# A fused block-causal attention and gated FFN kernel: the float32 first piece goes from 192 to 384 tokens, with q and k bounds on ScalarE and another DMA model in the planner

## The chip, the cores and the metric

The kernel runs on one core of a Trainium2 chip. TensorE (PE) does matrix products into PSUM, VectorE (DVE) and ScalarE (ACT) element-wise work and reductions, GpSimd (POOL) small element-wise work, and SyncE (SP) issues all DMAs. The metric is the device time of one execution in microseconds, lower is better. PEld in a profile is the loading of weights into TensorE, which runs beside its matmuls.

## What is computed

Eight sequences of 576 tokens go through attention with 8 heads of 64, masked by blocks of 64 tokens (a block of queries sees its own and all earlier blocks of keys). The heads are put side by side to 4608 x 512, and a feed-forward layer of width 2048 with the gate h * clip(h + 3, 0, 6) / 6 follows.

```python
scores = scale * np.matmul(q, k.transpose(0, 1, 3, 2))
mask = block_i >= block_j
scores = np.where(mask, scores, -1000000000.0)
scores = scores - np.max(scores, axis=-1, keepdims=True)
attn = np.exp(scores)
attn = attn / (np.sum(attn, axis=-1, keepdims=True) + 1e-09)
x = np.matmul(attn, v) ...
h = x @ w_in
g = h * np.clip(h + 3.0, 0.0, 6.0) / 6.0
return g @ w_out
```

q, k and v are float32. The two weights come as 64-bit numbers, which the kernel takes as pairs of 32-bit words.

## The kernel before

**Precision.** Most products are made from float16 pairs: an operand is scaled by a power of two and split into a high and a low float16 part, and three of the four partial products are summed (hi x hi, hi x lo, lo x hi). An f16 matmul covers half the output rows (64) and is issued in pairs for the two halves. The power of two comes from a bound on the operand's magnitude, made by `pow2_scale` (line 518) out of per-partition values in `mx`, which a matmul with ones sums over the partitions.

**The weights.** Each of the 8 chunks (`NCH`) of the two weight matrices is loaded in four quarters by `w_load` (594). Each quarter lies in one of three raw buffers and is turned to float32 in place by four operations: a sign (`sg`, line 622, VectorE or POOL), an exponent (`ex`, 623) and two bit operations on VectorE. `WX` (line 23) says up to which quarter the third raw buffer lies in x buffer 1, behind which it is `pT01`. The float32 form of chunk c lies where the f16 form of chunk c+1 will be, the last one in x buffers 2 and 3. `w_max` (637) finds the magnitudes and `w_split` (650) makes the f16 parts. A split of chunk c overwrites float32 weights of chunk c-1, so it comes behind the float32 FFN steps up to 2c (`splits`, line 1330).

**Batch 0 is computed in float32.** For each of its four pairs of heads, `qk_load32` and `qk_prep32` bring and transpose q and k, `s_block32` makes the scores of one block of 64 queries for both heads (matmul, maximum on VectorE, exponential on ScalarE), `t_block32` transposes the probabilities on TensorE and copies them out of PSUM, and `pv_group32` (940) does three blocks together: reciprocal sums, `rd` (36 multiplies of 64 columns in all, on POOL, line 948), a matmul `pr` that spreads them over partitions, a copy `rb`, the product with v and the scaling. The first group of three blocks (tokens 0 to 191, T0) of all four pairs goes to `x32`, float32; the other two groups (tokens 192 to 575) are split to f16 into x buffer 1.

**Batches 1 to 7** take f16 pairs: 28 slots, one for each batch and pair of heads (n = 4 to 31). `qk_prep` (758) finds the bounds of q and k with one maximum reduction (`absmax`, line 762) on VectorE, scales, splits and transposes by DMA. `s_group` (988) makes scores, maxima `st`, multiplies them with the scale (line 1033, VectorE), takes exponentials on ScalarE, splits the probabilities to `phl`, and a transposing DMA (`t_dma`) brings them to `pT`. `pv_group` (1102) multiplies with v and splits into x buffers.

**The FFN runs over pieces of tokens** (`pieces`, line 1088): piece 0 is (batch 0, tokens 0 to 191) in float32, piece 1 (0, 192 to 575), piece 2 (1, 0 to 383), piece 3 (1, 384 to 575), and then nine pieces of 384 tokens for six batches. A piece has 16 steps f of 128 hidden columns. `ffn1` makes `h` and the gate `g`, and `ffn2` adds to the accumulators `o0` to `o2` (one bank of PSUM for each 128 tokens), `LAG` (3) steps behind. In float32 a step is 4 products h over the piece's tokens, and one product of 512 columns for each 128 tokens, or two half-height ones of 256 columns for the last 64.

**What sets the order.** Nothing is emitted as it is called. A `Recorder` (line 84) notes every operation with its tiles and a due time `key`, and `schedule` (260) simulates the five engines with a cost formula (`cost`, 205), choosing at each engine's free moment the ready operation with the earliest due time; the resulting order is then fixed for each engine. A few operations may go to several engines ("AV" is ScalarE or VectorE, "VPA" any of three), and the planner chooses. Due times come from the constants at the top: `AS` and `U` for the first blocks of batch 0 and `TA`, `PV0` behind them, `RT`, `RS`, `TR` for the others, `W0 + i * WD` for the weight quarters, `S0`, `SD` for the splits, `AT` for the f16 slots and `FT` for the FFN pieces, with `PVA` and `PVB` placing the two value products of a slot. A DMA's landing is modelled in lines 423 to 426, where plain DMAs share one queue and transposes do not enter it.

PSUM has eight banks: three `s` (scores, value products, small matmuls), two `h`, and `o0` to `o2`, which the float32 attention also uses for transposes until the FFN needs them (`EVP`, `PRO`).

Of the kernel before, what the change touches and what calls it, by code (L numbers as in the profile page):

```python
# [17 lines left out]
P = 128  # L18
# [3 lines left out]
LAG = 3  # L22
WX = 10
WY = 27

U = 2.788
AS = (7.494, 11.408, 15.3, 22.633)
AL = 14.807
PV0 = 2.519
TA, TR, PR = 2.197, 5.661, 0.677  # L30
QR = 3.417
PVA, PVB = 0.93, 1.25
PHS = 18
# [4 lines left out]
EVR = 3  # L38
EVP = 2
PRO = True  # L40
MEM = 0

NMIN = 64
QL = 0.849
VL = 0.2
W0, WD = 4.938, 2.891
S0, SD = 57.576, 4.59
M0, MD = 34.073, 5
RT = (25.619, 42.369, 59.881, 71.242)
RS, RL, VL1 = 2.796, 15.216, 24.0  # L50
VM0, VMX = 10.452, 0.3
AT = ((4, 86.25), (6, 128.63), (8, 159.32), (10, 199.92), (12, 240.31), (14, 287.79), (16, 335.13), (24, 565.96), (32, 826.62))
FT = ((0, 28), (1, 100), (2, 168.81), (3, 239.13), (4, 279.57), (5, 356.87), (7, 505.16), (10, 740.96), (13, 988.23))
QP = 0.55
# [23 lines left out]

ADV = {("tensor", "a"): 60.0}


class Recorder:
# [4 lines left out]
    NAMES = ("tensor", "vector", "scalar", "gpsimd", "sync")  # L89
    LAT = {"tensor": 55, "vector": 37, "scalar": 39, "gpsimd": 65, "sync": 65}  # L90
    TURN = 95
    BIAS = {"vector": 250.0, "gpsimd": 500.0}
# [67 lines left out]
    def add(self, ways):  # L160
        eng, method, args, kw = ways[0]
        outs, ins = self.operands(args, kw)
        last = self.ops[-1] if self.ops else None
        if eng == "tensor" and self.joint is not None and last and last.joint == self.joint:
            op = last
            calls, occ, _, _ = op.ways[eng]
            more, took, _ = self.cost(eng, method, args, kw, outs, ins)
            op.ways[eng] = (calls + [(method, args, kw)], occ + more, occ + took, False)
        else:
            op = Op()  # L170
            op.joint, op.n, op.ways = None, len(self.ops), {}
# [12 lines left out]
    def touch(self, op, a, w):
# [18 lines left out]
        self.hist[t.name] = keep  # L203

    def cost(self, eng, method, args, kw, outs, ins):


        n = self.count(outs[0])
        if method == "dma_start":
            nb = mybir.dt.size(outs[0].dtype)  # L210
            for _, c in list(outs[0].ap):
                nb *= c
            if kw.get("transpose"):
                occ = max(1290, 172 * nb / 32768 - 150)
                return occ, occ + (1100 if nb <= 4 * 32768 else 2100), False
            if eng == "gpsimd":
                return 1300, 2900 + nb / 170, False
            return 600, 2000 + nb / 170, False
# [17 lines left out]
        if eng == "scalar":  # L236
            occ = 94 + 0.8335 * n
            if isinstance(kw.get("scale"), bass.AP):
                occ += 95
            if isinstance(kw.get("bias"), bass.AP):  # L240
                occ += 58
            if "accum_out" in kw:
                occ += 93
            return occ, occ + 105, False
        if eng == "gpsimd":
# [14 lines left out]
    def schedule(self):  # L260
# [63 lines left out]
        while done < N:  # L324
# [96 lines left out]
            while head < N and ops[head].start is not None:  # L421
                head += 1
            if calls[0][0] == "dma_start" and not calls[0][2].get("transpose"):
                nb = (took - (2900.0 if e == "gpsimd" else 2000.0)) * 0.8
                dma = max(dma, o.end - nb - 400.0) + nb
                o.end = max(o.end, dma + 400.0)
            now[e] = t + occ
# [7 lines left out]
            for s, flow in succ[pick]:  # L435
                rs = ready[s]
                for q in rs:
                    r = t if q == e and (e == "tensor" or not flow) else o.end + self.LAT[q]
                    rs[q] = max(rs[q], r)
                ndep[s] -= 1  # L440
                if not ndep[s]:
                    for q in rs:
                        heapq.heappush(pend[q], (rs[q], s))
# [12 lines left out]
def kernel(  # L456
# [31 lines left out]
    NGB, NPB, NST_B = ((4, 5, 4), (3, 6, 3), (3, 5, 5))[MEM]  # L488
    T0 = GT
    NTA, NTR = 2, 3  # L490

# [266 lines left out]
    def qk_prep(n):  # L758
        t = qn.pop(n)
        mx = sm.tile([P, 2], F32, tag="qkmx", name=f"qkmx{n}")  # L760
        sp = attp.tile([P, 3, NST, 2, D], F16, tag="qks", name=f"qks{n}", bufs=1)
        absmax(mx, t)
        pw, rs = pow2_scale(mx, 2, f"q{n}")
# [28 lines left out]
    def qk_load32(n):  # L792
        t = attp.tile([P, 2, NTA, 2, D], F32, tag="vhl", bufs=2, name=f"qf{n}")
        qn[n] = t
        for s, src in enumerate((q, k)):
            nc.sync.dma_start(t[:, s, 0], src[0, 2 * n:2 * n + 2, :P].rearrange("h p d -> p h d"))
            nc.sync.dma_start(
                t[:BLK, s, 1], src[0, 2 * n:2 * n + 2, P:T0].rearrange("h p d -> p h d")
            )

    def qk_load32_rest(n):
        t = natp.tile([P, 2, NTR, 2, D], F32, tag="qk", bufs=2, name=f"qr{n}")
        for s, src in enumerate((q, k)):
            for h in range(2):
                nc.sync.dma_start(
                    t[:, s, :, h], src[0, 2 * n + h, T0:].rearrange("(t p) d -> p t d", p=P)
                )
        qn[n] = t

    def qk_prep32(n, rest):  # L810
# [29 lines left out]
        for s in (1, 0):  # L840
            if rest and not QTH:
                ps = ps_s.tile([P, 512], F32, tag="s", name=f"qt{n}_{s}r")
            else:
                ps = ps_h.tile([P, S - T0], F32, tag="h", name=f"qt{n}_{s}")
            for u in range(NTR if rest else NTA):
# [62 lines left out]
    def t_block32(n, i):  # L908
# [7 lines left out]
        if ii == 0:  # L916
            tag = "pT2" if g or n in (1, 2) else "pT01"
            pT[n, g] = attp.tile(
                [P, PT_U[g], P], F32, tag=tag, bufs=2 if tag == "pT2" else 1, name=f"pT{n}_{g}"
            )  # L920
        t = pT[n, g]
        for u0 in range(0, nu, 4):
            u1 = min(u0 + 4, nu)
            full = u1 - 1 if half and u1 == nu else u1
            if g == 0 or EVP >> len(n_ev) % 3 & 1:
                o = 2 if g else len(n_ev) % 3
                pp = ps_o.tile([P, 4, P], F32, tag=f"o{o}", name=f"pt{n}_{i}_{u0}")
# [12 lines left out]
    def pv_group32(n, g):  # L940
# [6 lines left out]
        for i in range(GB):  # L947
            nc.gpsimd.tensor_scalar(rd[:, i], ident2, r[:, i:i + 1], 1.0, op0=ALU.mult, op1=ALU.mult)
        if g == 0 or PRO:
            o = 2 if g else len(n_ev) % 3  # L950
            pr = ps_o.tile([P, GT], F32, tag=f"o{o}", name=f"pr{n}_{g}")
# [5 lines left out]
        nc.scaled(rb, pr, 1.0, "AV")  # L957
        if g == 0:
            ps = ps_h.tile([P, GT], F32, tag="h", name=f"pf{n}_{g}")
        else:  # L960
            ps = ps_s.tile([P, GT], F32, tag="s", name=f"pf{n}_{g}")
        nj = (3 * g + 2) // 2 + 1
        for j in range(nj):
# [4 lines left out]
            for h in range(2):  # L968
# [6 lines left out]
                )  # L975
        if g == 0:
            nc.vector.tensor_mul(x32[:, n, :T0], ps, rb)
            return
        nc.vector.tensor_mul(rb, ps, rb)
        rs = vscale[0][1][:, 0:1]  # L980
        x = xb[1]
        xs = slice((g - 1) * GT, g * GT)
        nc.scaled(x[:, 0, n, xs], rb, rs, "AV")
# [4 lines left out]
    def s_group(n, g):  # L988
# [19 lines left out]
        for si, some in enumerate(banks):  # L1008
# [22 lines left out]
            if len(some) > 1:  # L1031
                nc.vector.tensor_tensor(st[:, 2:3], st[:, 2:3], st[:, 3:4], op=ALU.min)
            nc.vector.tensor_scalar_mul(st[:, 4 + i0:4 + i1], st[:, i0:i1], sc[:, 0:1])
            for ii, c0, c1, rg in regions:
# [52 lines left out]

    pieces = [[(b, *r)] for b in range(2) for r in ((0, (T0, TP)[b]), ((T0, TP)[b], S))]
    for b in range(2, B, 2):
        pieces += [[(b, 0, TP)], [(b, TP, S), (b + 1, 0, GT)], [(b + 1, GT, S)]]  # L1090
# [273 lines left out]
    for n in range(NPAIR):  # L1364
# [3 lines left out]
        at(t, qk_prep32, n, 0)  # L1368
        for i in range(GB):
            at(t + (1 + i) * U, s_block32, n, i)  # L1370
            at(t + (1 + i) * U + TA, t_block32, n, i)
        at(t + GB * U + TA + PV0, pv_group32, n, 0)

    for n in range(NPAIR):
# [3 lines left out]
        at(AS[3] + 0.1 + 0.1 * n, v_max, n)  # L1378
        for i in range(2 * GB):
            at(t + i * RS, s_block32, n, GB + i)  # L1380
            at(t + i * RS + TR, t_block32, n, GB + i)
        for g in (1, 2):
            at(t + (g * GB - 1) * RS + TR + PR, pv_group32, n, g)

# [88 lines left out]
```

## Time and profile before

| | |
|---|---|
| median of 3 runs | 1059.81 us (1059.1 to 1061.09) |
| span of the profiled execution | 1063.1 us |
| busy: PE | 995.4 us (94%), 11588 matmuls |
| busy: PEld | 726.0 us (68%) |
| busy: DVE | 833.9 us (78%) |
| busy: ACT | 635.8 us (60%) |
| busy: POOL | 75.9 us (7%) |
| mean granted TensorE clock | 0.980 |
| DMA share over the span | 61.4% of 16 engines, 127 MB |

In the profile, tiles are named as in the program with buffer numbers left out: `h`, `o`, `s`, `pv` are PSUM tiles of the matmuls; `sf`, `pt`, `pr`, `pf` those of the float32 attention; `pf` is also the name of its probabilities. All operations have the line of the recorder's caller (L452), so groups are told apart by tile and form. A form "128*64 128x384 f16" of a matmul is 128 rows by 64 columns of weights and 384 moving columns. A row of the list of waits reads: engine and tile that waited, what released it, us in total, times, longest. A row of a group reads: form and count, then busy us and mean ns of one, then idle time of the engine ahead of them and what ended most of it. A timeline row reads: start, length of the merged stretch, and in brackets idle time ahead and its releaser.

### The profile page before, as it was taken

The page shows a single profiled execution, that of the slowest core. Times are in us where ns is not written, and L with a number is a line of the kernel's source. Part 1 is how long each engine was busy: PE and PEld are TensorE (multiplying, and loading weights), DVE is VectorE, ACT ScalarE, POOL GpSimd, SP SyncE. Part 2 cuts the span into 40 slices and gives each one's busy share as a digit, 9 for nine tenths or more (in the row PEclk, how much of TensorE's full clock was granted, in tenths as well). Part 3 has the DMA queues.
Part 4 walks back from the last instruction along what each step waited for, and adds up shares of the span by engine and source line. Part 5 has one row for each costly group of instructions (what it writes and reads, how often), then busy time and mean ns, then how long its engine had stood idle before and what let it go on. Part 6 is the DMA issues. An engine that isn't in the chain of part 4 may idle for free. (4 is left out here: it accounts for less than half of the span.)

```text
span 1063.1 us, 28968 instructions
## 1 busy us (share of the span) xinstructions
PE 995.4 (94%) x11588; PEld 726.0 (68%) x11588; DVE 833.9 (78%) x2308; ACT 635.8 (60%) x1548; POOL 75.9 (7%) x259
## 2 busy tenths in 40 slices
PE   6978967999999999999999999999999999999998
PEld 4645646776777867667766666777767777777776
DVE  4888999999999999899899889787898875332322
ACT  4668757666657676666776565566556563343332
POOL 3132220000000000000000000000000000000000
PEclk8998988999999999999999999999999999999999
DMA  6756546898889887888888779647656533000000
GB/s 157 189 166 180 141 111 140 140 185 156 152 159 171 153 152 143 147 164 149 156 143 181 133 116 167 118 77 143 117 90 128 92 80 57 1 31 2 31 1 31
DMA packets 414199, 128.90 MB, mean 121 GB/s; under 512 B 403184, under 2 KB 403440, under 8 KB 414064
## 3 DMA queue, kind: packets, MB, share of 16 engines
q1 hardware_dynamic: 414064, 127.05, 61.4%
q8 instruction: 91, 1.49, 0.6%
q14 instruction: 44, 0.36, 0.1%
HBM read 45.09 MB, written 9.44 MB: 51 GB/s over the span
## 5 line engine op out<-in xcount | busy, mean ns | idle before, releaser
L452 PE MATMUL h<-x,win 128*64 128x384 f16 (+2 forms) x4720 | 437.0, 321 | 1.8 <-DVE win L452 1.6
L452 PE MATMUL o<-wout,g 128*64 128x512 f16 (+3 forms) x3444 | 430.9, 381 | 2.2 <-DVE g L452 2.2
L452 PEld LDWEIGHTS <-win 128*64 128x64 f16 x4608 | 296.8, 110 | 69.9 <-issue 2.2
L452 PEld LDWEIGHTS <-g 128*64 128x64 f16 x3360 | 221.6, 110 | 105.9 <-issue 2.0
L452 ACT ACTIVATE r<-h,eg,sh 128x384 f32<-128x384 f32 (+1 forms) x240 | 137.1, 593 | 131.5 <-PE h L452 130.8
L452 ACT ACTIVATE p<-s,st,esc 128x64 f32<-128x64 f32 (+1 forms) x280 | 163.1, 587 | 73.6 <-DVE st L452 53.6
L452 DVE SCALAR_TENSOR_TENSOR r<-r,eg,h 128x384 f32<-128x384 f32 (+1 forms) x192 | 113.4, 592 | 116.1 <-ACT r L452 116.0
L452 DVE SCALAR_TENSOR_TENSOR phl<-p,st,phl 128x128 f16<-128x128 f32 (+4 forms) x252 | 135.3, 582 | 0.7 <-ACT phl L452 0.6
L452 ACT ACTIVATE g<-r 128x384 f16<-128x384 f32 (+1 forms) x165 | 84.5, 513 | 85.8 <-DVE r L452 84.9
L452 DVE SCALAR_TENSOR_TENSOR g<-r,g 128x384 f16<-128x384 f32 (+1 forms) x192 | 102.7, 535 | 29.9 <-ACT g L452 29.4
L452 DVE TENSOR_REDUCE st<-s 128x1 f32<-128x64 f32 (+1 forms) x280 | 120.0, 447 | 4.1 <-PE s L452 3.8
L452 PE MATMUL s<-qkT 128*64 128x64 f16 (+7 forms) x1120 | 99.0, 289 | 10.0 <-ACT p L452 6.4
L452 PEld LDWEIGHTS <-vhl 128*64 128x64 f16 x1680 | 72.3, 111 | 41.2 <-issue 25.3
L452 PE MATMUL pv<-pT,vhl 128*64 128x192 f16 (+2 forms) x1680 | 75.1, 235 | 24.8 <-DMA pT<-phl 20.8
L452 ACT ACTIVATE phl<-p,st 128x256 f16<-128x256 f32 (+4 forms) x135 | 70.4, 556 | 34.4 <-DVE st L452 18.7
L452 PEld LDWEIGHTS <-qkT 128*64 128x64 f16 x1120 | 60.0, 111 | 35.4 <-issue 13.0
L452 POOL MEMSET p<- 128x64 f32 x140 | 21.4, 154 | 521.4 <-DVE phl L452 492.5
L452 ACT ACTIVATION_READ_ACCUMULATOR p<-s,st,esc 128x1 f32 x280 | 55.1, 197 | 0.0
L452 DVE TENSOR_SCALAR phl<-p,st 128x512 f16<-128x512 f32 (+4 forms) x117 | 46.0, 424 | 1.8
L452 DVE SCALAR_TENSOR_TENSOR qks<-qk,rs_q,qks 128x576 f16<-128x576 f32 x56 | 44.7, 817 | 0.0
L452 ACT ACTIVATE x<-pv 128x192 f16<-128x192 f32 (+1 forms) x61 | 22.0, 360 | 33.4 <-PE pv L452 30.7
L452 DVE TENSOR_REDUCE qkmx<-qk 128x2 f32<-128x1152 f32 x28 | 37.6, 1344 | 1.6 <-DMA qk<-in_k_dram 1.6
(154 smaller groups left out, 819.4 us busy)
## 6 DMA issues: line engine op xcount, KB each, us to landing
out_dram<-osb SPq DMA_DIRECT2D x35, 256.0 KB, 2.5
vnat<-in_v_dram SPq DMA_DIRECT2D x64, 128.0 KB, 2.9
qk<-in_q_dram SPq DMA_DIRECT2D x28, 288.0 KB, 3.6
qk<-in_k_dram SPq DMA_DIRECT2D x28, 288.0 KB, 4.4
rawo<-in_moe_w_out_dram SPq DMA_DIRECT2D x15, 512.0 KB, 4.6
rawi<-in_moe_w_in_dram SPq DMA_DIRECT2D x14, 512.0 KB, 4.0
pT<-phl SPq DMA_TRANSPOSE x140, 3.4
vnat<-in_v_dram SPq DMA_DIRECT2D x32, 32.0 KB, 2.7
```

The source lines that it names most:

```text
L452: getattr(eng, method)(*args, **kw)
```

## The change

The float32 piece takes two groups of three blocks of each pair instead of one: T0 is 384, and G32 = 2 counts those groups. Piece 0 is (0, 0 to 383), piece 1 the remaining 192 tokens of batch 0 in f16; the later pieces are the same. The first load of a pair brings three tiles of 128 tokens, the second 192 tokens, and the buffers of the two change places. The groups 0 and 1 of a pair share one `pT` tile; both use the `o` banks for transposes and `pr` and the `h` bank for the value product, the third group uses `s` banks alone. The x split remains for the third group. `rd` goes to ScalarE or VectorE. `qk_prep` takes the sum of magnitudes per partition, by two ScalarE passes with an accumulator, in place of one maximum on VectorE. The product of `st` and the scale may go to ScalarE or VectorE. The planner gets one queue for all DMAs, with lead, tail and rate for loads, stores and transposes; a matmul that reads what a DMA brings is planned 1250 ns behind its landing. The cost of an accumulating ScalarE pass grows by 90 ns in latency, and many due times are set anew. `WX` is 14, and the third group of a pair calls the loads up to that count first.

```diff
-WX = 10
+WX = 14
-U = 2.788
-AS = (7.494, 11.408, 15.3, 22.633)
-AL = 14.807
+U = 1.6
+AS = (7.5, 13, 18.5, 24)
+AL = 15.597
-TA, TR, PR = 2.197, 5.661, 0.677
-QR = 3.417
-PVA, PVB = 0.93, 1.25
+TA, TR, PR = 2.057, 5.661, 0.677
+QR = 2.99
+PVA, PVB = 0.863, 0.986
-EVP = 2
+EVP = 1
-S0, SD = 57.576, 4.59
-M0, MD = 34.073, 5
-RT = (25.619, 42.369, 59.881, 71.242)
-RS, RL, VL1 = 2.796, 15.216, 24.0
+S0, SD = 57.383, 4.623
+M0, MD = 34.073, 6.162
+RT = (36, 46.092, 56, 66.2)
+RS, RL, VL1 = 2.165, 23.579, 24.609
-FT = ((0, 28), (1, 100), (2, 168.81), (3, 239.13), (4, 279.57), (5, 356.87), (7, 505.16), (10, 740.96), (13, 988.23))
+FT = ((0, 34), (1, 120), (2, 165), (3, 235), (4, 275), (5, 350), (7, 500), (10, 739.72), (13, 984.72))
...
-ADV = {("tensor", "a"): 60.0}
+ADV = {("tensor", "a"): 97.06}
...
+    MARGIN = {"tensor": 1250.0}
+    QUEUE = {"load": (4137.0, -1860.0, 256.0), "store": (4137.0, -1860.0, 580.0), "turn": (4074.0, -2300.0, 182.0)}
...
+        kind = "turn" if kw.get("transpose") else "load" if self.on_chip(args[0]) else "store"
+        lead, tail, rate = self.QUEUE[kind]
+        return lead, tail, nb / rate
...
-            if calls[0][0] == "dma_start" and not calls[0][2].get("transpose"):
-                nb = (took - (2900.0 if e == "gpsimd" else 2000.0)) * 0.8
-                dma = max(dma, o.end - nb - 400.0) + nb
-                o.end = max(o.end, dma + 400.0)
+            margin = {}
+            if o.queue:
+                lead, tail, work = o.queue
+                dma = max(t + lead, dma) + work
+                o.end = dma + tail
+                margin = self.MARGIN
...
-                    r = t if q == e and (e == "tensor" or not flow) else o.end + self.LAT[q]
+                    r = t if q == e and (e == "tensor" or not flow) else o.end + self.LAT[q] + margin.get(q, 0.0)
...
-    T0 = GT
-    NTA, NTR = 2, 3
+    T0 = TP
+    NTA, NTR = 3, 2
+    G32 = 2
...
-        absmax(mx, t)
+        for s in range(2):
+            ab = sp[:, 1 + s].rearrange("p t l d -> p (t l d)").bitcast(BF16)[:, :NST * D]
+            nc.scalar.activation(
+                ab.rearrange("p (t d) -> p t d", d=D), t[:, s], AF.Abs, accum_out=mx[:, s:s + 1]
+            )
...
-            if g == 0 or EVP >> len(n_ev) % 3 & 1:
-                o = 2 if g else len(n_ev) % 3
+            if g < G32:
+                o = len(n_ev) % 3
...
-            nc.gpsimd.tensor_scalar(rd[:, i], ident2, r[:, i:i + 1], 1.0, op0=ALU.mult, op1=ALU.mult)
-        if g == 0 or PRO:
-            o = 2 if g else len(n_ev) % 3
+            nc.scaled(rd[:, i], ident2, r[:, i:i + 1], "AV")
+        if g < G32:
+            o = len(n_ev) % 3
...
-        if g == 0:
-            nc.vector.tensor_mul(x32[:, n, :T0], ps, rb)
+        if g < G32:
+            nc.vector.tensor_mul(x32[:, n, g * GT:(g + 1) * GT], ps, rb)
             return
+        while len(n_raw) < WX:
+            w_ops.pop(0)()
...
-            nc.vector.tensor_scalar_mul(st[:, 4 + i0:4 + i1], st[:, i0:i1], sc[:, 0:1])
+            nc.scaled(st[:, 4 + i0:4 + i1], st[:, i0:i1], sc[:, 0:1], "AV")
...
-    pieces = [[(b, *r)] for b in range(2) for r in ((0, (T0, TP)[b]), ((T0, TP)[b], S))]
+    pieces = [[(0, 0, TP)], [(0, TP, S)], [(1, 0, TP)], [(1, TP, S)]]
...
-        for i in range(GB):
+        for i in range(G32 * GB):
             at(t + (1 + i) * U, s_block32, n, i)
             at(t + (1 + i) * U + TA, t_block32, n, i)
-        at(t + GB * U + TA + PV0, pv_group32, n, 0)
+        for g in range(G32):
+            at(t + (g + 1) * GB * U + TA + PV0, pv_group32, n, g)
```

More of the change, by code (lines that the diff above doesn't have):

```diff
@@ L43 @@
 NMIN = 64
-QL = 0.849
-VL = 0.2
+QL = 1.222
+VL = 0.415
 W0, WD = 4.938, 2.891
-S0, SD = 57.576, 4.59
-M0, MD = 34.073, 5
-RT = (25.619, 42.369, 59.881, 71.242)
-RS, RL, VL1 = 2.796, 15.216, 24.0
-VM0, VMX = 10.452, 0.3
-AT = ((4, 86.25), (6, 128.63), (8, 159.32), (10, 199.92), (12, 240.31), (14, 287.79), (16, 335.13), (24, 565.96), (32, 826.62))
-FT = ((0, 28), (1, 100), (2, 168.81), (3, 239.13), (4, 279.57), (5, 356.87), (7, 505.16), (10, 740.96), (13, 988.23))
+S0, SD = 57.383, 4.623
+M0, MD = 34.073, 6.162
+RT = (36, 46.092, 56, 66.2)
+RS, RL, VL1 = 2.165, 23.579, 24.609
+VM0, VMX = 6.896, 0.388
+AT = ((4, 86.25), (6, 128.63), (8, 159.32), (9, 178.32), (10, 199.92), (12, 240.58), (14, 288.64), (16, 335.13), (24, 565.96), (32, 826.62))
+FT = ((0, 34), (1, 120), (2, 165), (3, 235), (4, 275), (5, 350), (7, 500), (10, 739.72), (13, 984.72))
+UNI = False
 QP = 0.55
@@ L61 @@
 class Op:
-    __slots__ = ("ways", "key", "preds", "joint", "n", "start", "end", "tiles", "eng", "half")
+    __slots__ = ("ways", "key", "preds", "joint", "n", "start", "end", "tiles", "eng", "half", "queue")
 class Engine:
@@ L175, in add @@
             op.preds, op.tiles, op.start = {}, [], None
+            op.queue = self.queue(args, kw) if method == "dma_start" else None
             op.half = eng == "tensor" and outs[0].ap[0][1] <= 64 and method == "matmul"
@@ L203, in touch, with queue @@
         self.hist[t.name] = keep
+    def queue(self, args, kw):
+        nb = mybir.dt.size(args[0].dtype)
+        for _, c in list(args[0].ap):
+            nb *= c
+        kind = "turn" if kw.get("transpose") else "load" if self.on_chip(args[0]) else "store"
+        lead, tail, rate = self.QUEUE[kind]
+        return lead, tail, nb / rate
     def cost(self, eng, method, args, kw, outs, ins):
@@ L213, in cost @@
             if kw.get("transpose"):
-                occ = max(1290, 172 * nb / 32768 - 150)
+                occ = max(1290, 189 * nb / 32768 - 200)
                 return occ, occ + (1100 if nb <= 4 * 32768 else 2100), False
@@ L243, in cost @@
                 occ += 93
+                return occ, occ + 195, False
             return occ, occ + 105, False
@@ L792, in qk_load32 @@
     def qk_load32(n):
-        t = attp.tile([P, 2, NTA, 2, D], F32, tag="vhl", bufs=2, name=f"qf{n}")
+        t = natp.tile([P, 2, NTA, 2, D], F32, tag="qk", bufs=2, name=f"qf{n}")
         qn[n] = t
[L795 to L802, printed above, removed]
         for s, src in enumerate((q, k)):
@@ L805, in qk_load32_rest @@
                 nc.sync.dma_start(
-                    t[:, s, :, h], src[0, 2 * n + h, T0:].rearrange("(t p) d -> p t d", p=P)
+                    t[:, s, :, h], src[0, 2 * n + h, :T0].rearrange("(t p) d -> p t d", p=P)
                 )
+    def qk_load32_rest(n):
+        t = attp.tile([P, 2, NTR, 2, D], F32, tag="vhl", bufs=2, name=f"qr{n}")
+        for s, src in enumerate((q, k)):
+            nc.sync.dma_start(t[:, s, 0], src[0, 2 * n:2 * n + 2, T0:T0 + P].rearrange("h p d -> p h d"))
+            nc.sync.dma_start(
+                t[:BLK, s, 1], src[0, 2 * n:2 * n + 2, T0 + P:].rearrange("h p d -> p h d")
+            )
         qn[n] = t
@@ L843, in qk_prep32 @@
             else:
-                ps = ps_h.tile([P, S - T0], F32, tag="h", name=f"qt{n}_{s}")
+                ps = ps_h.tile([P, T0], F32, tag="h", name=f"qt{n}_{s}")
             for u in range(NTR if rest else NTA):
@@ L916, in t_block32 @@
         if ii == 0:
[L917 to L920, printed above, removed]
+            if g != 1:
+                tag = "pT2" if g or n in (1, 2) else "pT01"
+                pT[n, g] = attp.tile(
+                    [P, PT_U[2], P], F32, tag=tag, bufs=2 if tag == "pT2" else 1, name=f"pT{n}_{g}"
+                )
+            if not g:
+                pT[n, 1] = pT[n, 0][:, PT_U[0]:]
         t = pT[n, g]
@@ L975, in pv_group32 @@
                 )
-        if g == 0:
-            nc.vector.tensor_mul(x32[:, n, :T0], ps, rb)
+        if g < G32:
+            nc.vector.tensor_mul(x32[:, n, g * GT:(g + 1) * GT], ps, rb)
             return
+        while len(n_raw) < WX:
+            w_ops.pop(0)()
         nc.vector.tensor_mul(rb, ps, rb)
@@ L981, in pv_group32 @@
         x = xb[1]
-        xs = slice((g - 1) * GT, g * GT)
+        xs = slice(0, GT)
         nc.scaled(x[:, 0, n, xs], rb, rs, "AV")
@@ L1083, in t_dma @@
         )
-    pieces = [[(b, *r)] for b in range(2) for r in ((0, (T0, TP)[b]), ((T0, TP)[b], S))]
-    for b in range(2, B, 2):
+    pieces = [[(0, 0, TP)], [(0, TP, S)], [(1, 0, TP)], [(1, TP, S)]]
+    if UNI:
+        pieces = []
+    for b in range(0 if UNI else 2, B, 2):
         pieces += [[(b, 0, TP)], [(b, TP, S), (b + 1, 0, GT)], [(b + 1, GT, S)]]
@@ L1378 @@
         at(AS[3] + 0.1 + 0.1 * n, v_max, n)
[L1379 to L1383, printed above, removed]
+        for i in range((NG - G32) * GB):
+            at(t + i * RS, s_block32, n, G32 * GB + i)
+            at(t + i * RS + TR, t_block32, n, G32 * GB + i)
+        at(t + ((NG - G32) * GB - 1) * RS + TR + PR, pv_group32, n, 2)
     for n in range(NPAIR, NSLOT):
```

## The prediction

> **What bounds the kernel now.** I read the page first, then busy time by stage, then the list of waits, then single stretches of the timeline. The profiled execution spans 1063.1 us; the runs have a median of 1059.81, 0.3% less. All sums are made against 1063.1 and multiplied by 0.9969 at the end.
>
> ```profile
> span 1063.1 us, 28968 instructions
> ```
>
> The stages, cut where the first FFN matmul starts and where the last weight split ends (columns: length, then busy time of PE, PEld, DVE, ACT, POOL with instruction counts, granted clock, DMA share, GB/s):
>
> ```profile
> 0.00:26.00 26.00, 17.81 (x72) 11.44 (x73) 11.29 (x34) 12.33 (x46) 9.71 (x36) 0.90 0.62 155
> 26.00:172.00 146.00, 120.09 (x733) 76.33 (x734) 130.97 (x352) 105.50 (x275) 37.27 (x64) 0.91 0.63 162
> 172.00:420.00 248.00, 237.68 (x3314) 182.97 (x3311) 239.84 (x714) 163.85 (x407) 11.57 (x62) 0.99 0.87 155
> 420.00:900.00 480.00, 460.52 (x5776) 335.33 (x5774) 404.17 (x1130) 298.12 (x720) 17.32 (x97) 0.99 0.69 126
> ```
>
> ```profile
> L452 PE MATMUL h<-x,win x4720: 243/326/689, 25.7 to 1051.2; 128*64 128x384 f16 x176, 128*64 128x192 f16 x16, 128*128 128x192 f32 x5
> L452 DVE SCALAR_TENSOR_TENSOR wout<-x,rsio,wout x2: 737/738/740, 171.5 to 172.1; 128x512 f16<-128x512 f32 x2
> ```
>
> From 172 us on TensorE is the bound: it idles 10.3 us up to 420 and 19.5 up to 900. Ahead of 172 it is not: it idles 8.2 us in the first 26 and 25.9 up to 172, while VectorE is 90% busy there with converting and splitting the weights. The list of waits says what those idle microseconds are:
>
> ```profile
> PE pv L452 <- DMA pT<-phl: 20.8, 20, 2.5
> PE pr L452 <- POOL rd L452: 8.3, 5, 2.9
> PE pt L452 <- ACT pf L452: 8.3, 6, 6.1
> PE s L452 <- ACT p L452: 6.4, 6, 3.3
> ```
>
> The first is the f16 attention waiting for the transposing DMA of the probabilities; it lies wholly behind 172 us, where those operations exist. The second and third belong to the float32 attention of batch 0. And there is a second loss that no wait list shows, stretches at half clock:
>
> ```profile
> 21.00:27.80 6.80, 6.18 (x24) 3.70 (x24) 1.97 (x5) 2.76 (x9) 0.26 (x1) 0.50 0.94 291
> 61.90:65.30 3.40, 3.40 (x13) 2.33 (x12) 2.49 (x6) 2.89 (x9) 0.15 (x1) 0.51 0.12 12
> 79.00:89.20 10.20, 7.39 (x20) 5.02 (x21) 7.66 (x20) 7.15 (x18) 3.48 (x7) 0.50 0.37 107
> ```
>
> Each comes right around a wait for rd:
>
> ```profile
> 21.31 1.01 PE L452 MATMUL pr<-rd,halves 128*128 128x192 f32 x2 [1.49 <-POOL rd L452]
> 60.57 0.59 PE L452 MATMUL pr<-rd,halves 128*128 128x192 f32 x2 [2.93 <-POOL rd L452]
> 79.47 1.01 PE L452 MATMUL pr<-rd,halves 128*128 128x192 f32 x2 [2.68 <-POOL rd L452]
> ```
>
> **Part 1: 192 more tokens in float32.** Each float32 product is two matmuls (seven of the eight weight chunks, 56 products, make 112), and the price of one is taken from starts that follow each other at full clock:
>
> ```profile
> L452 PE MATMUL h<-x,win 128*128 128x192 f32 x112 | 25.9, 360 | 1.8 <-DVE win L452 1.6 <-DVE x L452 0.3
> ```
>
> ```profile
> 102.77 0.49 PE L452 MATMUL pt<-ident,pf 128*128 128x128 f32 x3
> 103.15 0.27 PE L452 MATMUL mt_w<-ident,wm 128*2 128x128 f32 x1
> 103.26 1.14 PE L452 MATMUL h<-x,win 128*128 128x192 f32 x6
> 104.24 1.02 PE L452 MATMUL o<-wout,g 128*128 128x512 f32 x2
> 105.09 1.02 PE L452 MATMUL sf<-qkf 128*128 128x512 f32 x2
> 106.25 0.65 PE L452 MATMUL o<-wout,g 128*64 128x256 f32 x4
> 106.84 0.43 PE L452 MATMUL h<-x,win 128*128 128x192 f32 x1
> ```
>
> Six float32 h matmuls take 103.26 to 104.24, 0.163 us each, 0.85 ns a column.  Two o matmuls over 512 columns take 0.85, four half-height ones 0.59. With 192 tokens one of the 16 steps is 8 x 0.163 + 0.85 + 0.59 = 2.74 us, the piece 43.9. With 384 the h matmuls double in width (8 x 0.326) and there are three full o tiles (3 x 0.85): 5.16, the piece 82.5. The other side, f16:
>
> ```profile
> 1045.66 1.95 PE h L452 x24
> 1047.61 1.94 PE o L452 x18
> 330.78 1.18 PE L452 MATMUL h<-x,win 128*64 128x192 f16 x24
> 331.77 1.49 PE L452 MATMUL o<-wout,g 128*64 128x512 f16 x12
> ```
>
> A step of 384 tokens costs 1.95 + 1.94 = 3.89, the piece 62.2. A step of 192 costs 0.99 for h (330.78 to 331.77), and for o one and a half of three tiles, 0.97: 1.96, the piece 31.4. TensorE gets 38.6 us and loses 30.8: **+7.8 us** of work on the bounding engine. The ends are close (a 384-wide h lies between 0.163 and 0.43): +6 to +10.
>
> The prologue changes as well. Before, FFN starts at 25.7 us behind 12 blocks; after, 24 blocks must end first, with pieces up to 384 keys. TensorE work of a pair: score columns 448 before and 1408 after, times two matmuls times 0.85 ns, are 0.8 and 2.4; transposes (0.127 us each by the row at 102.77) 8 and 18, 1.0 and 2.3; normalizer and value product about 0.8 and 2.0 (estimates at 0.85 ns a column). Four pairs: 10 and 27 us. What sets the end is ScalarE and VectorE:
>
> ```profile
> L452 ACT ACTIVATE pf<-sf,st 128x64 f32<-128x64 f32 x4 | 1.3, 315 | 3.6 <-DVE st L452 3.6
> L452 ACT ACTIVATE pf<-sf,st 128x384 f32<-128x384 f32 x4 | 2.3, 580 | 0.9 <-DVE st L452 0.5 <-DVE pw_q L452 0.4
> L452 ACT ACTIVATE pT<-pt 128x384 f32<-128x384 f32 x7 | 3.4, 488 | 2.0 <-PE pt L452 2.0
> L452 DVE TENSOR_REDUCE st<-sf 128x1 f32<-128x320 f32 x8 | 3.8, 475 | 0.3 <-PE sf L452 0.2
> L452 ACT ACTIVATE exo<-rawo 128x512 f32<-128x512 f32 x14 | 9.4, 673 | 2.6 <-DVE sums L452 2.6
> L452 DVE SCALAR_TENSOR_TENSOR sgo<-rawo,sgo 128x512 uint32<-128x512 uint32 x15 | 10.9, 729 | 0.0
> qr<-in_q_dram SPq DMA_DIRECT2D x8, 96.0 KB, 4.9
> qf<-in_q_dram SPq DMA_DIRECT2D x4, 64.0 KB, 2.2
> ```
>
> Per pair, estimated between those rows: six exponentials at 0.45 plus their sums (0.2), seven copies of transposes at 0.37, three of q and k at 0.49, two of rb at 0.33, six rd at 0.3, about 10.3 us; six maxima at 0.38 and small ones, 3.8. Four pairs 56 us. The last pair's second group is due at 24 + 6 x 1.6 + 2.06 + 2.52 = 38, and by then twelve weight quarters are (W0 + i x WD), each 0.67 on ScalarE and some 1.6 on VectorE: 27. Together 83 us on two engines; at the 81% at which both ran between 26 and 172 us that is 52 us; with nothing lost, 42. SyncE's first loads grow too: before, 64 KB landed in 2.2 us; the new ones are 96 KB like those that took 4.9, so about 2.6 later, four issues a pair either way. I put the first FFN matmul at 52 us. Before, TensorE had 10 us of work in 25.7 (some 16 unused); after, 27 in 52 (25 unused): **+9**, ends 0 and +20.
>
> What this buys: between 26 and 172 us TensorE idled 25.9 us, 6.8 of it for rd. The remaining 19 are VectorE being late. Now 38.6 us more matmuls that need only unsplit weights are at hand in that stage, so most of it is filled: **-15**, ends 0 and -19. VectorE's own load there hardly moves (the float32 step needs one multiply, the f16 step two more passes), so it stays beside TensorE's work. Against it: the new piece takes all three o banks, so in the last three blocks of each pair transposes and normalizers share three s banks with the scores; and a split of chunk c is held by the float32 o steps up to 2c (line 1330), queued behind twice the matmuls. Both are inside the end 0.
>
> **Part 2: rd off POOL.** The 36 multiplies of line 948 go to ScalarE or VectorE.
>
> ```profile
> L452 POOL TENSOR_SCALAR rd<-ident,sums x36: 313/320/2799, 10.7 to 147.5; 128x64 f32<-128x64 f32 x36
> ```
>
> On POOL one takes 0.32 at the median and 2.8 at worst, and three stand in a row ahead of pr; the 64-wide exponential (0.315) is the nearest row for ScalarE. The wait of 8.3 us shrinks to the queue in front of ScalarE: **-6.5**, ends 0 and -8.3. POOL's queue is then left with its memsets. Those half-clock stretches held 17 us of busy time, half of it lost: **-6**, ends 0 and -8.5. The Trainium skill, page "TensorE: Matmul & The Clock Gate", part 1, has the clock fall only after an idle window of about 3.4 us; by that rule none of these waits (2.93 the longest) lowers it, this term is nil and the sum 6 us higher. The trace disagrees: 0.50 was granted around each of the three.
>
> **Part 3: bounds as sums on ScalarE, bias on either.**
>
> ```profile
> L452 DVE TENSOR_REDUCE qkmx<-qk 128x2 f32<-128x1152 f32 x28 | 37.6, 1344 | 1.6 <-DMA qk<-in_k_dram 1.6
> L452 ACT ACTIVATE abi<-win 128x512 f32<-128x512 f32 x14 | 8.7, 624 | 3.7 <-DVE win L452 3.2 <-DVE rsio L452 0.2
> ```
>
> VectorE loses 28 x 1.34 = 37.6 us. ScalarE gains 56 passes; by the 512-wide one plus a read of the sum about 0.88 each, 49 us. From 172 to 900 us ScalarE is 63% busy and would be some 70%: its idle time hides this, 0 on the path. If that cover were gone, the chain of one pair would grow by 0.4 us ahead of its scores, 12 us in all.
>
> **Part 4: one fitted DMA queue.** This changes only the order that the planner writes: a matmul that reads what a DMA brings is planned 1.25 us after the modelled landing, and transposes now stand in the queue. So TensorE gets other matmuls ahead of pv, and FFN matmuls are there in plenty until 900 us. Of the 20 waits of 20.8 us (about 1 us each, 2.5 at most) I take off **-13**, with VectorE's relief helping the copies ahead of the DMA. Ends: -19, and +3, since pv's own due times come earlier (0.93 to 0.863, 1.25 to 0.986 of a slot) and could draw it ahead of its data. What is late next is the wait of s for ScalarE (6.4).
>
> **The sum.** 7.8 + 9 - 15 - 6.5 - 6 - 13 = -23.7: 1039.4 of the profiled span, times 0.9969 = **1036 us**.
>
> **The rivals.** *Slower, 0.14:* the prologue is the price. If ScalarE and VectorE run it at two thirds, FFN starts at 63 us (+20), VectorE is as late as before behind it (0 for the fill), rd waits in ScalarE's queue instead (-2), the clock stays, and the DMA waits give 10: 7.8 + 20 - 2 - 10 = +16, or 1076. For it: in the first 26 us both engines were under half busy, bound by latency. Against: twice the blocks in flight. It decides where the first 384-wide float32 matmul starts: behind about 76 us (52 and the 24 that the forecast gains) nothing is left. Half way between the forecast and it lies 1056.
>
> *The fill fails alone, 0.14:* VectorE stays the bound up to the last split; without the -15 the result is 1051.
>
> *The order does not act, 0.07:* pv waits for its DMA as before, since a planned time isn't kept by late engines; without the -13, 1049.
>
> *The clock stays low, 0.05:* other waits of the longer prologue hold it at 0.50 as long as before; without the -6, 1042. That is what the page's rule would give for a removal of these waits.
>
> **How the numbers follow.** The forecast has 0.60. Its own range, the unknown costs moving apart, is 1016 to 1056. The range of 1012 to 1060 takes in the smaller failures and the milder half of the slower rival, and leaves out some 0.07 below (all terms near their good ends) and 0.11 above. A change within 0.2% (2 us, about what a measurement of this kernel can tell) needs a bit over half of the slower rival (0.02) or two failures at once (0.03): 0.05. Slower: the rest of its rival, 0.12. Faster: 0.60 + 0.14 + 0.07 + 0.05 less those 0.03, 0.83.
>
> **What would show it.** In the profile after: first FFN matmul near 52 us; idle of TensorE from there to the last split under 10 us; rd on ScalarE and VectorE, no wait for POOL above 1 us; less than 15 us at clock 0.50 ahead of the last split; pv waiting for DMA under 10 us in all; qkmx gone from VectorE and ScalarE near 690 us busy. I am wrong if the f16 work behind the last split isn't about 31 us shorter, or if the last split comes more than 30 us later than at 172.

## The result and the profile after

The changed kernel takes **1014.78 us** (median of 4, 1013.83 to 1015.16); the kernel before, on the same chip, 1060.45. The ratio is 0.9557 (95% interval 0.952 to 0.9593): 4.4% faster, 46 us by the medians, where 1036 us and 24 us were forecast. The page and the stages, cut as before (length; busy time of PE, PEld, DVE, ACT, POOL; granted clock; DMA share; GB/s):

```profile
span 1013.4 us, 28806 instructions
PE 986.8 (97%) x11492; PEld 710.9 (70%) x11492; DVE 788.3 (78%) x2177; ACT 695.5 (69%) x1794; POOL 54.1 (5%) x219
```

```profile
0.00:26.00 26.00, 20.98 (x120) 15.03 (x120) 17.72 (x55) 18.02 (x62) 7.19 (x30) 1.00 0.84 208
26.00:172.00 146.00, 143.81 (x761) 77.40 (x763) 140.89 (x392) 121.60 (x325) 19.73 (x35) 1.00 0.65 163
172.00:420.00 248.00, 236.24 (x3501) 184.72 (x3499) 228.01 (x687) 195.07 (x532) 11.28 (x64) 0.99 0.94 164
420.00:900.00 480.00, 476.27 (x5951) 351.65 (x5949) 369.61 (x992) 322.52 (x808) 15.90 (x90) 1.00 0.67 119
900.00:1013.00 113.00, 109.55 (x1172) 82.11 (x1168) 32.02 (x55) 38.26 (x70) 0.00 (x0) 1.00 0.04 15
```

Read down the PE column. From 26 to 172 us TensorE now idles 2.2 us where it idled 25.9, at a clock of 1.00 instead of 0.91; from 420 to 900 it idles 3.7 instead of 19.5. From 172 to 420 it idles 11.8, a little more than the 10.3 before. And the stretch behind 900 us, FFN alone, is 50 us shorter: that is where time saved earlier comes out. The list of waits, and the last split:

```profile
PE s L468 <- ACT p L468: 7.0, 10, 2.5
PE qt L468 <- DMA qf<-in_q_dram: 3.7, 1, 3.7
PE pv L468 <- DMA pT<-phl: 2.8, 4, 1.2
PE pr L468 <- DVE rd L468: 0.3, 1, 0.3
```

```profile
L468 DVE SCALAR_TENSOR_TENSOR wout<-x,rsio,wout x2: 747/747/747, 163.0 to 167.4; 128x512 f16<-128x512 f32 x2
```

The waits for the transposing DMA (20.8) and for rd (8.3) are all but gone; the largest left is that of the scores for ScalarE (7.0, 6.4 before). The last split ends at 168 us instead of 173, though the float32 piece ahead of it has twice the tokens.

Span, idle time and half-clock time of TensorE account for it. The span shrank by 49.7 us; idle time fell from 67.7 to 26.6 (41.1); busy time fell by 8.6, although the FFN's matmuls cost some 9 more. Most of the fall in busy time is the clock: in the trace's record of the granted clock the stretches at 0.50 add up to 41 us before (seven) and to 3.4 after (one), without one at the very end of each execution. The same three numbers for every kernel that ran (us, worked out from the PE busy time and the clock of its trace):

| kernel | median | ratio to before | span | PE idle | clock 0.50 |
|---|---|---|---|---|---|
| before | 1060.45 | | 1063.1 | 67.7 | 41 |
| b_rd | 1063.2 | 0.9982 (0.9955 to 1.0008) | 1061.9 | 62.6 | 48 |
| b_sums | 1064.39 | 0.9993 (0.9971 to 1.0015) | 1063.8 | 64.3 | 44 |
| b_queue | 1030.66 | 0.9666 (0.9625 to 0.9707) | 1027.7 | 39.8 | 27 |
| b_three | 1027.6 | 0.9635 (0.959 to 0.9679) | 1026.9 | 39.1 | 27 |
| a_oldqueue | 1043.35 | 0.9834 (0.9796 to 0.9872) | 1040.5 | 49.0 | 14 |
| a_nomargin | 1023.93 | 0.9664 (0.9625 to 0.9702) | 1022.3 | 34.4 | 10 |
| a_rdpool | 1022.96 | 0.9644 (0.9614 to 0.9674) | 1023.2 | 30.8 | 14 |
| a_absmax | 1024.74 | 0.9653 (0.9618 to 0.9688) | 1025.2 | 31.8 | 20 |
| a_margin2500 | 1021.21 | 0.9604 (0.9552 to 0.9656) | 1020.2 | 31.2 | 7 |
| a_last_first | 1019.0 | 0.9578 (0.9516 to 0.964) | 1019.7 | 30.6 | 7 |
| a_nudge1 | 1014.33 | 0.9542 (0.9491 to 0.9593) | 1012.1 | 24.7 | 7 |
| a_nudge2 | 1012.31 | 0.9526 (0.9474 to 0.9579) | 1009.3 | 21.2 | 3 |
| **changed** | **1014.78** | 0.9557 (0.952 to 0.9593) | 1013.4 | 26.6 | 3 |

The kernel before varied more between the jobs (medians 1060.5 to 1064.6) than the changed ones, so ratios are compared where they come from different jobs. The four kernels whose names begin with b ran in the job with 1064.58. Their expectations are reckoned from 1059.81, so the times named there are to be read through the ratio.

### The profile page after: what moved, and what is told of

Read it like the earlier page. It is cut to its first block, busy times and chain, and to the rows that moved or that the text cites. A ratio compares the mean times of both kernels' runs of the same rounds, so it can differ in the third digit from the quotient of the medians.

```text
span 1013.4 us, 28806 instructions
## 1 busy us (share of the span) xinstructions
PE 986.8 (97%) x11492; PEld 710.9 (70%) x11492; DVE 788.3 (78%) x2177; ACT 695.5 (69%) x1794; POOL 54.1 (5%) x219
## 4 chain that ended last, share of the span: by engine, by line
PE 45%; DVE 5%; ACT 1%; DMA 1%; issue 1%; SPq 0%; DVEq 0%; ACTq 0%
PE o L468 20%; PE h L468 20%; PE s L468 3%; PE pv L468 2%; DVE phl L468 1%; DVE st L468 1%; DVE r L468 1%; DVE g L468 1%; DVE qks L468 1%; DMA pT<-phl 0%; ACT p L468 0%; DMA vnat<-in_v_dram 0%; DVE x L468 0%; ACT osb L468 0%; DVE vmax L468 0%
## 5 line engine op out<-in xcount | busy, mean ns | idle before, releaser
L468 PE MATMUL o<-wout,g 128*64 128x512 f16 (+2 forms) x3348 | 431.6, 379 | 0.0
L468 PEld LDWEIGHTS <-win 128*64 128x64 f16 x4608 | 287.3, 110 | 69.6 <-issue 7.5
L468 PEld LDWEIGHTS <-g 128*64 128x64 f16 x3264 | 213.7, 110 | 99.2 <-DVE g L468 0.2
L468 ACT ACTIVATE r<-h,eg,sh 128x192 f32<-128x192 f32 (+1 forms) x240 | 134.3, 581 | 116.9 <-PE h L468 116.2
L468 DVE SCALAR_TENSOR_TENSOR g<-r,g 128x384 f16<-128x384 f32 (+1 forms) x192 | 99.6, 520 | 33.4 <-ACT g L468 32.2
L468 ACT ACTIVATE g<-r 128x384 f16<-128x384 f32 (+1 forms) x149 | 73.7, 495 | 66.4 <-DVE r L468 65.4
L468 ACT ACTIVATE phl<-p,st 128x128 f16<-128x128 f32 (+4 forms) x128 | 66.4, 550 | 17.4 <-DVE st L468 7.8
L468 ACT ACTIVATE st<-st,esc 128x1 f32<-128x1 f32 (+2 forms) x133 | 38.2, 291 | 40.7 <-DVE st L468 40.0
L468 DVE TENSOR_SCALAR phl<-p,st 128x384 f16<-128x384 f32 (+4 forms) x124 | 48.7, 422 | 2.1
L468 ACT ACTIVATE qks<-qk 128x576 bf16<-128x576 f32 x56 | 37.8, 679 | 7.9 <-DMA qkT<-qks 7.9
```

The source lines that it names most:

```text
L468: getattr(eng, method)(*args, **kw)
```

## The experiments

**One part alone on the kernel before.** First rd:

```diff
-            nc.gpsimd.tensor_scalar(rd[:, i], ident2, r[:, i:i + 1], 1.0, op0=ALU.mult, op1=ALU.mult)
+            nc.scaled(rd[:, i], ident2, r[:, i:i + 1], "AV")
```

> The kernel before with one part of the change alone: rd on ScalarE or VectorE in place of POOL. Theory (the waits for rd cost their own time and the clock behind them): 8.3 us of waiting and half of 17 busy us at half clock come back, 1043 to 1048 us, and the stretches at clock 0.50 around 21, 62 and 79 us are gone. Rival 1 (the clock does not hang on these waits): 1052, the stretches stay. Rival 2 (ahead of 172 us VectorE is the bound, so the waits move elsewhere): 1057 to 1060, TensorE's idle time in that stage stays near 34 us.

No change can be measured: the second rival held (0.9982 of 1059.81 is 1058, and TensorE idles 32.5 us ahead of 172). The stage from 26 to 172 us of b_rd, its waits there, and one stretch of TensorE's timeline:

```profile
26.00:172.00 146.00, 120.47 (x716) 75.74 (x716) 132.73 (x364) 108.53 (x288) 20.30 (x33) 0.91 0.62 161
```

```profile
PE pt L452 <- ACT pf L452: 6.7, 2, 6.5
PE o L452 <- DVE g L452: 5.2, 2, 3.0
PE pr L452 <- ACT rd L452: 1.4, 1, 1.4
```

```profile
77.28 0.59 PE L452 MATMUL pr<-rd,halves 128*128 128x192 f32 x2 [1.39 <-ACT rd L452]
78.07 0.92 PE L452 MATMUL h<-x,win 128*128 128x192 f32 x4 [0.20 <-DVE win L452]
81.96 2.08 PE L452 MATMUL o<-wout,g 128*128 128x512 f32 x2 [2.97 <-DVE g L452]
```

The wait for rd in that stage is 1.4 us instead of 6.8, and TensorE idles 25.5 instead of 25.9. Where 2.68 us were waited for rd at 79.5 us, 2.97 are now waited for VectorE's g at 82, and a stretch at half clock again lies around it (6.8 us from 81.1; 10.2 from 79.0 before). VectorE is 91% busy there; the wait has changed its name.

Then the DMA queue of the planner, with its margin (the lines of the change from `MARGIN` to `margin.get`, and the transposes' cost):

> The kernel before with the new DMA queue in the planner and its 1250 ns margin alone; due times as before. Theory (the order is what keeps TensorE from waiting for transposes): pv's waiting for DMA falls from 20.8 to under 8 us, 1044 to 1050 us. Rival (a planned landing isn't kept by engines that run late): the waiting stays over 15 us, 1056 to 1062.

The gain is 3.3%, 34 us by the medians, more than twice the theory's (10 to 16). The two stages behind 172 us in b_queue and its wait for transposes:

```profile
172.00:420.00 248.00, 247.46 (x3446) 191.16 (x3444) 246.38 (x739) 167.68 (x419) 11.48 (x63) 1.00 0.95 162
420.00:900.00 480.00, 474.73 (x5968) 344.53 (x5963) 403.05 (x1129) 291.27 (x698) 17.88 (x94) 1.00 0.67 121
PE pv L466 <- DMA pT<-phl: 0.5, 1, 0.5
```

Idle time from 172 to 900 us falls from 29.8 to 5.8 us: the 20 us of pv, and the s waits with them. The clock stays at 1.00 there, and the last split ends at 165 us instead of 173. Ahead of 172 TensorE still idles 30 us.

Then the sums and the bias (code shortened):

```diff
-        absmax(mx, t)
+        for s in range(2):
+            nc.scalar.activation(ab..., t[:, s], AF.Abs, accum_out=mx[:, s:s + 1])
-            nc.vector.tensor_scalar_mul(st[:, 4 + i0:4 + i1], st[:, i0:i1], sc[:, 0:1])
+            nc.scaled(st[:, 4 + i0:4 + i1], st[:, i0:i1], sc[:, 0:1], "AV")
```

> The kernel before with the q and k bounds as sums on ScalarE and the scaled st on either engine alone. Theory (VectorE is off the path behind 172 us and ScalarE has room): 1054 to 1061. Rival (VectorE at 97% from 172 to 420 us makes the probabilities late, and its relief is what shortens the waits for the transposing DMA): pv's waiting falls from 20.8 to under 12 us, 1045 to 1050.

No change, as the theory had it (0.9993 of 1059.81 is 1059). pv's waits do fall, to 13.4 us, but scores then wait 6.4 us for the transposed q and k, 1.0 before.

All three together, with the float32 piece still at 192 tokens:

> The kernel before with rd, sums and queue together, but the float32 piece still 192 tokens and all due times as before. Theory (the larger float32 piece is a cause of its own, filling TensorE ahead of the last split): 1028 to 1038, and 15 to 25 us stay for the piece. Rival (these three give it all, the piece only moves work): 1013 to 1020. In the first case TensorE still idles 15 us or more ahead of the last split.

The three parts multiply to 0.964 and give 0.9635 together: 1021 of 1059.81, between the two bands, while the median itself, 1027.6, is next to the theory's. TensorE idles 25 us ahead of 172 us, as the theory had it. So **the queue alone gives three quarters of the gain** (undone in the changed kernel, below, it costs 63% of it). The step from here to the changed kernel, the larger piece with its due times, gives 0.8% by the ratios, 8 us (their intervals just touch), and 12.8 us by the medians of the two jobs: less than the theory's 15 to 25 either way. The piece and its due times were not run apart. What they remove together is in the first two stages. Before, b_three, and the changed kernel, each from 0 to 50 and from 50 to 172 us:

```profile
0.00:50.00 50.00, 40.33 (x197) 26.18 (x198) 30.58 (x90) 27.46 (x92) 12.68 (x45) 0.93 0.69 176
50.00:172.00 122.00, 97.58 (x608) 61.59 (x608) 111.68 (x295) 90.37 (x230) 34.30 (x56) 0.90 0.61 155
```

```profile
0.00:50.00 50.00, 41.13 (x193) 27.58 (x194) 34.69 (x101) 31.56 (x107) 7.70 (x30) 0.90 0.74 199
50.00:172.00 122.00, 105.47 (x714) 66.59 (x714) 115.56 (x319) 96.97 (x260) 28.22 (x41) 0.93 0.61 155
```

```profile
0.00:50.00 50.00, 42.78 (x248) 28.00 (x249) 40.79 (x126) 39.16 (x132) 8.18 (x33) 1.00 0.84 214
50.00:172.00 122.00, 122.00 (x634) 64.43 (x634) 117.82 (x321) 100.46 (x255) 18.75 (x32) 1.00 0.61 152
```

From 50 to 172 us b_three idles 16.5 us at clock 0.93; the changed kernel not at all, at 1.00. VectorE is 95 and 97% busy: it is as full as before, but TensorE now has matmuls to run beside it. Behind 172 us something was lost again: up to 420 TensorE idles 0.5 us in b_queue, 7.2 in b_three and 11.8 in the changed kernel, where 6.3 of them are scores that wait for ScalarE. Which part brings this is not shown.

**One part undone in the changed kernel.** The old DMA model:

> The changed kernel with the old DMA model in the planner (plain DMAs in one queue, transposes outside it, no margin); all else as changed. Theory (the order that the DMA model gives is the largest single part, with or without the larger float32 piece): 25 to 36 us come back, 1040 to 1052 us, with over 12 us of pv waiting for transposes behind 172 us. Rival (the new due times carry the order as well): under 1028, pv waiting under 8 us.

The theory held: 28.6 us come back, and pv waits 14.4 us again:

```profile
PE pv L466 <- DMA pT<-phl: 14.4, 20, 2.1
```

Next the margin alone:

```diff
-    MARGIN = {"tensor": 1250.0}
+    MARGIN = {}
```

> The changed kernel with the fitted queue but no margin of 1250 ns. Theory (the margin covers engines that run later than planned, and is what matters): 1030 to 1045 us and pv waiting for transposes above 10 us. Rival (the transposes' place in one queue is what matters, their times are then right): 1015 to 1022.

```profile
PE pv L468 <- DMA pT<-phl: 15.3, 14, 2.1
```

Neither held whole. pv waits 15.3 us, as the theory said, but the time is 9 us longer and not 15 to 30. So the margin is what removes the waits of pv, and the queue's times without it still give two thirds of the part. They do so by other waits: scores wait 0.9 us for ScalarE instead of the 7.5 under the old model, and TensorE's idle time falls from 49.0 to 34.4 us in all.

```diff
-            nc.scaled(rd[:, i], ident2, r[:, i:i + 1], "AV")
+            nc.gpsimd.tensor_scalar(rd[:, i], ident2, r[:, i:i + 1], 1.0, op0=ALU.mult, op1=ALU.mult)
```

> The changed kernel with rd back on POOL. Theory (ahead of the last split TensorE now has other matmuls to run while rd is made): 1014 to 1019 us, waits for rd under 3 us. Rival (rd on POOL costs its waits and a clock at 0.50 behind them): 1023 to 1030 and stretches at 0.50 ahead of 100 us.

8.2 us slower, beyond the theory's band and at the edge of the rival's, but not by rd's waits: they are 0.2 us. The last split ends at 173 us instead of 168, and 10 us more run at half clock, 6.8 of them from 83.5 us, where the rival had them. POOL's pass over a sign (`sgo`) takes 1250 ns on the mean instead of 864. Which of these leads to the others isn't settled.

> The changed kernel with the maximum of q and k on VectorE again and the scaled st on VectorE alone. Theory (neither engine sets the end while TensorE has FFN matmuls to run): 1013 to 1019 us. Rival (with TensorE 97% busy, VectorE's 38 us more between 110 and 800 us make it late): 1022 to 1032, idle time of TensorE behind 172 us above 25 us (15.5 + 3.5 now).

10 us slower (the maximum and the scaled st back on VectorE alone): the rival's time, with less idle time than it asked for (22.4 us behind 172). Idle time grows by 5.2 us over the whole span and the half-clock time by 17; busy time grows by 6.6.

**Is it scatter?** Every undoing above gives a new planned order, for which the due times were not fitted.

> The changed kernel with one due time nudged and nothing else: RS 2.165 to 2.2, the spacing of the last blocks of batch 0. No operation, engine choice rule or cost changes. Theory (a planned order scatters: any small edit of a fitted set of due times gives another order, worth several us, and the 8 to 10 us of the single undoings of rd, of sums and of the margin lie within that): 1018 to 1028 us. Rival (those undoings cost what they cost by themselves): 1013 to 1017.

> The changed kernel with another due time nudged: QP 0.55 to 0.56, the lead of q and k of the f16 slots. Theory (scatter of the planned order): off by 3 us or more from 1014.8, to either side, mostly slower since the set was fitted. Rival (undoings cost what they cost): within 2 us of 1014.8.

The theory of scatter is not borne out, but only one of the two kernels tests it. In the trace of a_nudge1 every engine runs the same instructions in the same order as in the changed kernel: RS moved nothing, and 1014.33 only shows how well the time repeats in another job. QP left the order alone up to 183 us and moved 16% of the matmuls in all (those outside the longest sequence that both orders share). It gave 1012.31, 2.5 us off, between what the two sides asked for. Undoing rd moves 18%, the margin 19% and the sums 25%, each already ahead of 50 us. The two edits that follow move 20 and 17%, put nothing of the kernel before back, and cost 6 and 4 us. So the 8 to 10 us of the single undoings are more than any of these, but how much of them is the part itself, and how much is due times that no longer fit, is not shown. a_nudge2 is the fastest kernel here; its interval (0.9474 to 0.9579) doesn't separate it from the changed one.

```diff
-    MARGIN = {"tensor": 1250.0}
+    MARGIN = {"tensor": 2500.0}
```

> The changed kernel with a margin of 2500 ns in place of 1250. Theory (the margin covers engines that run later than planned, and 1250 covers nearly all of it): pv's waiting for transposes 0 to 2.8 us, time 1014 to 1026, no gain beyond the scatter of the order. Rival (the remaining idle time of TensorE is lateness that a larger margin takes): 1005 to 1012.

Slower by 6 us, and pv has no wait for transposes left to remove. Of 0, 1250 and 2500 ns the middle one is best, with the due times of the changed kernel in all three.

**The prologue.**

```diff
-        for d in range(NDT):
+        for i, d in enumerate((3, 0, 1, 2)):
```

> The changed kernel with the four products of the float32 h in the order of pairs 3, 0, 1, 2 in place of 0 to 3, so that no FFN matmul can start until the last pair's six blocks are done. Theory A (the early pairs' h products are what fills TensorE until 50 us): TensorE idles 3 us or more beyond the 7.2 it idles now ahead of 50 us, 1017 to 1022 us. Theory B (the blocks 6 to 8 of the first pairs fill it): under 2 us more there, the time within the scatter that the nudged kernels show. The step of the prediction (25 us unused by then) would need 15 us or more idle there.

The float32 h matmuls of the first 60 us, first in the changed kernel and then in this one, and the first 50 us of this one:

```profile
L468 PE MATMUL h<-x,win x30: 486/486/590, 26.0 to 59.0; 128*128 128x384 f32 x30
```

```profile
L468 PE MATMUL h<-x,win x25: 486/486/927, 49.3 to 59.8; 128*128 128x384 f32 x25
0.00:50.00 50.00, 41.09 (x241) 27.75 (x242) 40.37 (x129) 40.22 (x134) 7.50 (x32) 0.99 0.86 219
```

With the first h held back from 26.0 to 49.3 us TensorE idles 8.9 us instead of 7.2: theory B by the idle time. The time, 4 us longer, lies in theory A's band and beyond the 2.5 us of a_nudge2, by intervals that overlap. What fills the prologue is seen in the changed kernel's timeline:

```profile
41.03 0.92 PE L468 MATMUL sf<-qkf 128*128 128x448 f32 x2
42.08 0.91 PE L468 MATMUL h<-x,win 128*128 128x384 f32 x2
44.37 1.56 PE L468 MATMUL sf<-qkf 128*128 128x512 f32 x4
49.30 3.49 PE L468 MATMUL h<-x,win 128*128 128x384 f32 x10 [0.59 <-DVE x L468]
```

Scores over 448 and 512 keys are blocks 6 and 7, of the group that the first FFN step doesn't need. At 49.3 us the last pair's x arrives, and h runs.

## Why the prediction was right, and where it was not

The range held, but with luck. The measured time lies 2.8 us inside the low end of 1012 to 1060 and outside the forecast's own range of 1016 to 1056; the gain is nearly twice the 24 us of the forecast. Of the signs that the prediction named, all but the first came: the first FFN matmul was at 26.0 us, not near 52. Term by term:

- **What bounds which stage** held. Ahead of the last split VectorE is 90% busy before and 97% after, and taking rd's waits away there gave nothing; TensorE bounds the rest.
- **The price of 192 more float32 tokens**, +7.8 us: by the busy time of the groups of h and o, float32 went from 58.2 to 96.5 (+38.3, forecast +38.6) and f16 from 819.1 to 790.0 (-29.1, forecast -30.8), so +9.2.
- **The prologue**, +9 us, failed. The first two h matmuls came at 26.0 us, since a product over pair d needs only that pair. It was so before, too: the h matmuls at 25.7 us, which the prediction took for the start of the FFN, belong to the first two pairs, and those of the last pair came at 39.8:

```profile
39.77 0.59 PE L452 MATMUL h<-x,win 128*128 128x192 f32 x2 [0.27 <-DVE x L452]
```

Like for like, the first complete step moved from 39.8 to 49.3 us. The 49.3 is near the forecast 52, but the forecast set its 25 unused us up to there against 16 up to 25.7, which is another point of the work. The step that failed is "after, 27 in 52 (25 unused)". It gave TensorE only 24 blocks until then, where blocks 6 to 8 of the first pairs were run ahead. Idle time up to 50 us is 7.2 us; before it was 9.7, in b_three 8.9.

- **The fill**, -15, was right and somewhat small: 24.4 us of idle time from 50 to 172 became none, 16.5 of them by the piece with its due times (from b_three on).
- **rd and the clock behind it**, -6.5 and -6, failed as a part of their own: alone, rd gave nothing. VectorE was 90% busy in that stage, which the first view had shown; the wait taken from TensorE there was waited for elsewhere (idle 25.5 us for 25.9). The clock came back with another part: b_three still has 27 us at half clock, the changed kernel none ahead of 172 us. Before, the four stretches from 21.0 to 147.2 us were 27 us with 21 of busy time, half of which, 10 us, was lost.
- **The sums**, 0, held on the kernel before, and ScalarE came to 695.5 us for the forecast 690. In the changed kernel undoing them costs 10 us, part of which may be due times that no longer fit. VectorE is then 97% busy from 172 to 420 us instead of 92%, and TensorE idles 15.0 us there instead of 11.8. "Its idle time hides this" was said of ScalarE; what VectorE's 38 us are worth once TensorE has little other idle time was not asked.
- **The queue**, -13, was mis-sized: it measured 34 alone and 29 when undone. I took two thirds of pv's 20.8 us. It took all but 0.5 us of the waits, and with them went waits of s, two stretches at half clock behind 172 us, and 8 us from the last split.

By the ratios, on 1060 us, rd, sums and queue together gave 39 us where their terms, rd, clock and queue, came to 25.5. The larger piece with its due times gave another 8 where its terms (7.8 + 9 - 15) came to a loss of 1.8. (By the medians of the two jobs the two gains are 37 and 12.8.) So what the forecast lacked has two places: the queue's term, too small by some 20 and offset by rd and the clock, too large by 10; and the prologue's, which cost no idle time at all. None of the rivals happened in the changed kernel; in b_rd the clock did stay low, as the last of them had it.

## What to carry to other kernels

Before a removed wait is put into a sum, ask which engine bounds that stage: where it is another one, the wait can come back under another name, as rd's did. In a kernel whose order is planned ahead, the model of DMA landings is a lever of its own: with every DMA in one queue and a margin of about one wait's length, 20 us of stalls went behind matmuls that were there anyway. Work that needs nothing of the bounding engine can be worth more than its price ahead of a bottleneck: 9 us of dearer matmuls, with due times set for them, went with 16 us less idle time and a full clock. And before a small edit is taken as a test of scatter, compare the two orders in the traces: one of the two nudges here had changed nothing.

## What the runs showed of the hardware

The clock. The prediction tied the half clock to the waits for rd. b_rd has no such wait above 1.4 us and 48 us at half clock, so rd was not the cause. What does stand ahead of most falls is a stretch of about 3.4 us in which TensorE was busy for less than half of it, with no single long wait needed. The 3.4 us ahead of five falls in the kernel before (at 21.0, 61.9, 79.0, 437.4 and 587.6 us), of one in b_rd and of the one in the changed kernel:

```profile
17.60:21.00 3.40, 1.41 (x7) 0.58 (x5) 3.11 (x8) 2.17 (x11) 1.09 (x3) 1.00 0.75 163
58.50:61.90 3.40, 1.33 (x5) 0.81 (x6) 1.72 (x4) 0.70 (x2) 2.01 (x3) 1.00 0.48 154
75.60:79.00 3.40, 1.19 (x9) 0.39 (x8) 3.40 (x10) 2.40 (x5) 2.60 (x2) 1.00 0.58 178
434.00:437.40 3.40, 1.37 (x19) 0.75 (x20) 3.40 (x11) 1.34 (x2) 0.31 (x1) 1.00 0.39 86
584.20:587.60 3.40, 0.88 (x26) 0.83 (x26) 3.37 (x13) 1.44 (x2) 0.41 (x2) 1.00 0.34 65
```

```profile
77.70:81.10 3.40, 1.10 (x6) 0.62 (x4) 3.40 (x9) 3.03 (x9) 1.74 (x2) 1.00 0.62 207
```

```profile
239.70:243.10 3.40, 1.14 (x22) 1.01 (x24) 1.40 (x5) 3.06 (x9) 0.31 (x1) 1.00 0.87 195
```

TensorE was busy for 0.9 to 1.4 us of the 3.4 each time, and the half clock then lasted 3.4 us or a multiple of it (17 us once in b_rd). The Trainium skill, page "TensorE: Matmul & The Clock Gate", part 1, gives a window of that length and asks for it to be idle; the length agrees, but a window that is partly busy was enough here. The threshold was not measured.

Within one execution all these stretches lie on a grid of 3.41 us, so that the traces of all 14 kernels can be cut into such windows. Of 45 falls, 42 follow a window in which TensorE was busy for 0 to 54%; three, in the first 48 us of b_rd, b_three and a_nomargin, follow windows of 65 to 70% and are not explained. Behind the first 4 us every window at full clock with a share under 43% was followed by half clock. Between 43 and 54% both happened.
